# One Trainium2 core, a state-space layer beside a Mish layer: layer-norm statistics moved behind size maxima, and half of the C copies, weight scalings and weight sums moved to other places of the instruction order

## The chip, the cores and the metric

The kernel runs on one core of a Trainium2 chip. The time is the device time of one execution in microseconds (us), and lower is better. Five engines work side by side, each through its own list of instructions in order: TensorE (PE, matmuls into eight PSUM banks), VectorE (DVE), ScalarE (ACT), GpSimd (POOL) and SyncE (SP, which only issues DMAs here). ACT and POOL issue DMAs too. An instruction that waits holds up everything behind it on its engine.

## The reference

x has 2048 rows of 1024 values. It is normalized by row, and the result goes through two branches that are added to x: a diagonal complex recurrence with input matrix B and output matrix C (1024 states), and a dense layer to 3584 features with Mish, followed by a dense layer back to 1024.

```python
xn = _layernorm(x, axis=-1)
# state-space branch
Lam_bar = jnp.exp(dt * Lam)
B_bar = ((Lam_bar - 1.0) / Lam)[:, None] * Bmat
Bu = jnp.einsum("bld,pd->blp", xn + 0j, B_bar)
for t in range(L):
    h = Lam_bar[None, :] * h + Bu[:, t, :]
y = 2.0 * jnp.einsum("blp,dp->bld", hseq, Cmat).real + xn * Dskip[None, None, :]
# dense branch
h = jnp.einsum("bsd,df->bsf", xn, w1) + b1
act = h * jnp.tanh(softplus(h))
return x + y + jnp.einsum("bsf,fd->bsd", act, w2)
```

## The kernel before

**Blocks.** The 2048 rows are worked in four blocks of 512 (`blk` 0 to 3). Each block has the same stages on TensorE: dense 1 (28 tiles f of 128 features, `first_tile`, L816, one PSUM bank per tile, f modulo 8), the projection with B (`project_in` in block 0, `project_fast` later), dense 2 (`dense`, called in `tail`, L1182), and the projection with C (`proj`, L1182 too), whose output units are added to x and stored (`finish`, L1251; `store`, L1243).

**Fast products.** From block 1 on the B projection uses sums of blocks of the operands in place of some products, so that seven products of half size do the work of eight (`product`, L880). For blocks 2 and 3 dense 1 does the same with W1 (`w_product`, L950). This needs scaled copies and sums of the weights, in float16, made while blocks 0 and 1 run.

- For W1 there are seven groups of 512 features, 0 to 6. `w_load(i)` (L1024) has POOL load group i raw, four DMAs into the scratch buffers `hb` or `act`. `w_scale(i)` (L1085) has ACT scale it in place by two activations, and POOL store three of the four pieces to DRAM (`w_store`, L1079). `w_sums(i)` (L1097) has VectorE form four sums, each stored by POOL. The scale comes from size maxima: for groups 3 to 6 VectorE reads the ring of weights in block 0 (`w_most`, L1044) and `w_row(0)` spreads them; groups 0 to 2 are measured by ACT in block 1 (`w_abs`, L1035, `w_row(1)`).
- For B and C the scale of each state comes from sizes of B (`rows_size`, `rows_scale`). `rows_C(j)` (L1341, its store L1343) has ACT write a scaled copy of row group j of C into four tiles of `act` and then store that to DRAM, from ACT's own DMA queue. `scale_B` (L1350) and `sums_B` (L1361, L1362) have VectorE scale B and form its sums, which are written over the memory of the C rows that have been copied.

**The order.** Every engine's list is written out by hand. The call order in the Python code is the order on each engine; a helper (`Queue`, `Buf`) derives the semaphore waits from what each operation reads and writes. `side(f)` is called after the tile f of dense 1 and puts other work there. The strings HEAD, HEAD1, WHOLE and SEVEN hold the order of a later block's projection, one word for each step: a letter a to d with a digit is a product of a pair of row groups and its evacuation, r a rotation, u the first matmuls of a unit of dense 2, k `w_sums`, n `w_load`. Block 1 uses WHOLE, blocks 2 and 3 SEVEN.

**Statistics.** x of block 1 is loaded by POOL during block 0's dense 1; `ln_stats_only` (L517, L519) forms mean and variance of a quarter of it on VectorE, four calls. They are needed when the first recurrence of block 0 is done (`ln_root`).

**Weights and the ring.** W1, W2 and the scaled C come through a ring of seven slots filled by SP (L408, L411). A slot is refilled when TensorE, and in block 0 `w_most`, have read it. SP also issues the transposing loads of B (L793) and C (L799), in order with the ring's loads.

**The recurrence.** `recur` (L1147 to L1157) runs on VectorE, eight row groups in a block; in block 0 VectorE and ACT also scale a row group of C behind each (`scale_C`, L780 to L787).

Of the kernel before, what the change touches and what calls it, by code (L numbers as in the profile page):

```python
# [163 lines left out]
def build_kernel(nc, A_x, A_Lambda_re, A_Lambda_im, A_B_re, A_B_im, A_C_re, A_C_im,  # L164
# [9 lines left out]
    NJ = NP // P  # L174
# [6 lines left out]
    FAST = 1  # L181
# [1 line left out]
    SPLIT = range(2, NB)  # L183
    GROUPS = ((0, 7), (7, NPL), (NPL, NPL + 8), (NPL + 8, NF))
    HEAD = "a2 a1 b2 b1 a5 b5 a6 b6 a3 b3 a7 b7 c2 d2 a4 b4 c5 c1 r0 d5 d1 r1 c6 c3 d6"
    HEAD1 = HEAD.replace("a2 a1 b2 b1", "k5 a2 a1 b2 b1 k6").replace("c6 c3", "n0 n1 c6 c3")
    WHOLE = HEAD1 + " d3 c7 d7 u7 c4 r2 u5 d4 u6 u4 r3 r4 r5 r6 r7"
    LATE = (" a3 b3 a7 b7 c2 d2 a4 b4 c5 c1 d5 d1 c6 c3 d6"
            " d3 c7 w1 d7 w5 w2 c4 d4 w6 r0 x1 x5 x2 w7 w3 r1 x6 w4 y1 y5 y2 x7 x3 r2 y6 x4"
            " z1 z5 g2 z2 y7 y3 z6 y4 u0 z7 u2 z3 u1 z4 u7 g3 r3 r4 r5 r6 r7")  # L190
# [109 lines left out]
    def wsm(n, lo, hi):  # L300
        return cs[:, CN.index("den") + n, lo:hi]
# [212 lines left out]
    def ln_stats_only(blk, q):  # L514
        i, s = blk % 2, q % 2
        for h in range(2):
            vop(lambda e, h=h: e.bn_stats(stats[:, s, h, :], xx[:, i, q, h * 512:(h + 1) * 512]),  # L517
                reads=[b_xx[i][q]], writes=[b_stats[s]])
        vop(lambda e: e.bn_aggr(mv[:, q, :], stats[:, s, :, :]), reads=[b_stats[s]], writes=[b_mv[q]])  # L519
# [497 lines left out]
    def w_load(i):  # L1017
        sem = DmaSem(nc, "d_wraw%d" % i, nper=4)
        for ci in range(2):
            for kh in range(2):  # L1020
                dst, b_dst = w_unit(w_raw(i, ci, kh))
                f0 = (4 * i + 2 * ci) * P
                src = B_w1[kh * NH * P:(kh + 1) * NH * P, f0:f0 + 2 * P].rearrange("(k p) f -> p k f", p=P)
                PO.dma(lambda e, dst=dst, src=src: e.dma_start(dst.rearrange("p (k f) -> p k f", k=NH), src),  # L1024
                       sem, writes=b_dst)
# [56 lines left out]
    def w_scale(i):  # L1082
        for ci in range(2):
            t, b_t = w_half(i, ci)
            aop(lambda e, t=t: e.activation(t, t, AF.Copy, scale=wsm(2, i, i + 1)),  # L1085
                reads=b_t + [b_wsm[2][i]], writes=b_t)
        for n, ci, kh in ((1, 0, 0), (2, 0, 1), (4, 1, 1)):
            w_store(i, n, *w_unit(w_raw(i, ci, kh)))
# [12 lines left out]
    def project_fast(blk, order, open_unit):  # L1101
        keep = {}
        split = order is not WHOLE
        for o in order.split():
            kind, n = o[0], int(o[1:])
            if kind == "r":
                rotate_in(n)
            elif kind == "u":
                open_unit(n)
            elif kind == "g":  # L1110
                mish(blk, n)
            elif kind == "k":
                w_sums(n)
            elif kind == "n":
                w_load(n)
            elif kind in QUADS:
                w_product(blk, QUADS.index(kind), n)
                w_evacuate(blk, QUADS.index(kind), n, keep)
            else:
                product("abcd".index(kind), n)  # L1120
                evacuate("abcd".index(kind), n, keep, split or kind in "ab")
# [257 lines left out]
    for blk in range(NB):  # L1379

        def side(f):
            if blk:
                at = (8, 10, 12, 15)
                if f in at:
                    ln_skip(blk, at.index(f))
                    if blk >= FAST:
                        sums_x(at.index(f))
                if blk == FAST:
                    if f == 1:
                        rows_spread(1)  # L1390
                    if f == 0:
                        scale_B(0, (1,))
                    if f < 3:
                        scale_B(f + 1)
                    if f in (3, 4, 17, 19):
                        sums_B((3, 4, 17, 19).index(f))
                    if f == 4:
                        w_scale(4)
                    if f in (7, 11):
                        w_sums(3 + (f - 7) // 4)  # L1400
                    if f == 16:
                        w_load(5)
                        w_load(6)
                    if f in (21, 24):
                        w_scale(5 + (f - 21) // 3)
                return
            if f == 2:
                turn_sines()
            if f == NR:
                aop(lambda e: e.activation(act[:, 0:NR, 0:2 * P], hraw[:, 0:NR, :], AF.Mish),  # L1410
                    reads=b_hbf[0:4], writes=b_actf[0:NR])
            if f in (19, 27):
                for j in range(4):
                    table(j + (4 if f > 19 else 0))
            if f in (5, 6, 7, 8):
                coefficients(f - 5)
            if f in (8, 9, 11, 12):
                ln_skip(0, (8, 9, 11, 12).index(f))
            if f in (14, 16, 18, 20):
                ln_stats_only(1, (f - 14) // 2)  # L1420
            if f in turns:
                transpose_B(turns.index(f))
            if f >= 26:
                transpose_C(f - 26)
            if f >= 4 * ROWS[0][0] and f % 4 < 2:
                w_most(f // 4, f % 4)
            if f == 26:
                w_row(0)

        for f in range(0 if blk in SPLIT else NF):  # L1430
            first_tile(blk, f)
            side(f)

        near = 0 < blk < NB - 1
        out_stage = tail(blk, n_item[0] + (len(W_ITEMS) if blk in SPLIT else 0))
        open_unit = next(out_stage)
        if blk in SPLIT:
            if near:
                for q in range(NQ):
                    load_x(PO, blk + 1, q)  # L1440
            project_fast(blk, SEVEN, open_unit)
        elif blk:
            project_fast(blk, WHOLE, open_unit)
        else:
            project_in()
        if near and blk not in SPLIT:
            for q in range(NQ):
                next_stats(blk + 1, q)
            w_abs(0)
            w_abs(1)  # L1450
        for j in range(NJ):
            if blk == 0 and j == NJ - 1:
                rows_scale(0)
            recur(blk, j)
            if near and j == (5 if blk in SPLIT else 1):
                next_root()
                for q in range(NQ):
                    next_scale(blk + 1, q)
            if blk in SPLIT:
                if j == 1:  # L1460
                    next(out_stage)
                if near and j == 1:
                    for q in range(NQ):
                        next_stats(blk + 1, q)
                if near and j == 5:
                    for q in range(NQ):
                        transpose_dma(q)
                continue
            if blk:
                if j == 1:  # L1470
                    next(out_stage)
                    w_load(2)
                    w_abs(2)
                    w_row(1)
                if j == 6:
                    w_exponent(1)
                    for i in (0, 1, 2):
                        w_scale(i)
                continue
            if j == 0:  # L1480
                ln_root()
                w_exponent(0)
                for q in range(NQ):
                    ln_scale(1, q)
                next(out_stage)
                for i in range(NHS):
                    rows_load(i)
            scale_C(j)
            for i in {4: (0, 1, 2), 5: (3, 4, 5, 6), 6: (7, 8, 9, 10), 7: range(11, 16)}.get(j, ()):
                rows_size(i)  # L1490
        if near:
            for q in range(NQ):
                ln_skip(blk + 1, q)
            for n in range(4):
                sums_x(n, VE)
        if blk < NB - 1:
            carry()
        if blk == FAST:
            for i in (0, 1, 2):
                w_sums(i)  # L1500
        if blk == FAST - 1:
            rows_scale(1)
            vop(lambda e: e.tensor_tensor(qi[:], qi[:], c("ss").unsqueeze(1).to_broadcast([P, 2, NJ]), op=ALU.mult),
                reads=[b_qi] + b_ss, writes=[b_qi])
            rows_spread(0)
            scale_B(0, (0,))
            for j in range(NJ):
                rows_C(j)
            for i in (3, 4):
                w_load(i)  # L1510
            w_scale(3)
        for _ in out_stage:
            pass
        if blk == FAST - 1:
            snaps_ready()

    SP.wait(out_events.values())

# [33 lines left out]
```

## Time and profile before

| what | us |
|---|---|
| median of 3 runs (618.35 to 621.8) | 619.75 |
| the profiled execution | 617.87 |
| its span, first to last instruction | 616.3 |
| TensorE busy | 601.0 |
| VectorE busy | 476.8 |
| ACT busy | 278.6 |
| POOL busy | 122.6 |
| mean granted TensorE clock | 0.992 of full |

A busy TensorE is not TensorE at its peak, since matmuls are pipelined; the granted clock of a stretch says whether it ran at full speed. The stages of block 0 and 1 on TensorE, by the first matmul of each:

| stage | starts at |
|---|---|
| block 0, dense 1 (full tiles) | 21.91 |
| block 0, projection with B | 58.17 |
| block 0, dense 2 | 85.79 |
| block 0, projection with C | 135.59 |
| block 1, dense 1 | 163.61 |
| block 1, projection with B | 217.99 |
| block 1, dense 2 (after the first units) | 252.53 |

Over the whole span 132.95 MB are moved by DMA, a mean of 216 GB/s.

### The profile page before, as it was taken

The page shows a single profiled execution, that of the slowest core. Times are in us where ns is not written, and L with a number is a line of the kernel's source. Part 1 is how long each engine was busy: PE and PEld are TensorE (multiplying, and loading weights), DVE is VectorE, ACT ScalarE, POOL GpSimd, SP SyncE. Part 2 cuts the span into 40 slices and gives each one's busy share as a digit, 9 for nine tenths or more (in the row PEclk, how much of TensorE's full clock was granted, in tenths as well). Part 3 has the DMA queues.
Part 4 walks back from the last instruction along what each step waited for, and adds up shares of the span by engine and source line. Part 5 has one row for each costly group of instructions (what it writes and reads, how often), then busy time and mean ns, then how long its engine had stood idle before and what let it go on. Part 6 is the DMA issues. An engine that isn't in the chain of part 4 may idle for free.

```text
span 616.3 us, 9311 instructions
## 1 busy us (share of the span) xinstructions
PE 601.0 (98%) x3583; PEld 349.3 (57%) x3583; DVE 476.8 (77%) x748; ACT 278.6 (45%) x367; POOL 122.6 (20%) x162
## 2 busy tenths in 40 slices
PE   8999999999979979999999999999999999999998
PEld 7644444444434448544448888644446888844444
DVE  6958998999978747989994667599954577689923
ACT  4749604479876362693615615590303714620000
POOL 2899200220327744100251000000000000000000
PEclk9999999999999979999999999999999999999999
DMA  9996999992699986268999707765576805864421
GB/s 244 295 229 181 193 220 248 307 293 80 183 377 384 335 311 203 81 227 183 265 364 366 271 18 223 229 181 167 159 206 220 307 18 157 254 202 141 163 76 68
DMA packets 109669, 132.95 MB, mean 216 GB/s; under 512 B 54346, under 2 KB 69322, under 8 KB 109626
## 3 DMA queue, kind: packets, MB, share of 16 engines
q1 hardware_dynamic: 97168, 95.77, 54.1%
q0 software_dynamic: 8768, 28.26, 13.6%
q10 hardware_dynamic: 3690, 8.34, 3.6%
q8 instruction: 28, 0.46, 0.3%
q14 instruction: 15, 0.12, 0.1%
HBM read 99.04 MB, written 21.24 MB: 195 GB/s over the span
## 4 chain that ended last, share of the span: by engine, by line
PE 59%; DVE 16%; DMA 9%; SPq 6%; POOL 5%; issue 3%; ACT 2%; ACTq 0%; POOLq 0%; DVEq 0%
PE ps L1182 37%; PE ps L950 12%; PE ps L880 11%; SPq L799 4%; DVE hT L1147 3%; DMA xx<-in_A_x_dram 2%; DVE CT L787 2%; DMA wsd<-hb 2%; DVE CT L784 2%; DMA out_dram<-xx 2%; ACT snaps L970 2%; DVE hb L1097 2%; DVE mt L1152 1%; DVE cs L1044 1%; POOL py L709 1%
## 5 line engine op out<-in xcount | busy, mean ns | idle before, releaser
L1182 PE MATMUL ps<-ring,act 128*128 128x512 bf16 x704 | 153.2, 379 | 1.2 <-DVE mt L1133 1.2
L1182 PEld LDWEIGHTS ps<-ring,act 128*128 128x128 bf16 x704 | 68.8, 98 | 84.0 <-issue 1.7
L816 PE MATMUL ps<-xnT,ring 128*128 128x512 bf16 x392 | 86.8, 384 | 4.4 <-ACT act L824 4.2
L970 ACT ACTIVATE snaps<-ps,par,cs 128x256 f32<-128x256 f32 x80 | 43.3, 562 | 99.6 <-PE ps L950 49.9
L1182 PE MATMUL ps<-ring,hT 128*128 128x512 bf16 x378 | 82.1, 379 | 0.0
L816 PEld LDWEIGHTS ps<-xnT,ring 128*128 128x128 bf16 x392 | 38.6, 99 | 52.2 <-issue 7.6
L1182 PEld LDWEIGHTS ps<-ring,hT 128*128 128x128 bf16 x378 | 37.0, 98 | 44.6
L1147 DVE TENSOR_TENSOR_SCAN hT<-cs,qi,hT 128x512 bf16<-128x512 f32 x48 | 58.9, 1268 | 0.0
L950 PE MATMUL ps<-TT,ring 128*128 128x256 f16 x448 | 55.8, 273 | 0.4 <-ACT snaps L970 0.4
L950 PEld LDWEIGHTS ps<-TT,ring 128*128 128x128 f16 (+1 forms) x448 | 43.7, 98 | 6.8 <-issue 0.9
L1182 PE MATMUL ps<-ring,hb 128*128 128x512 bf16 x192 | 43.1, 379 | 0.5 <-DVE act L973 0.5
L950 PE MATMUL ps<-xnT,ring 128*128 128x256 bf16 x336 | 42.9, 273 | 0.0
L824 ACT ACTIVATE act<-ps,par 128x512 bf16<-128x512 f32 (+1 forms) x56 | 33.8, 670 | 19.1 <-PE ps L816 19.1
L1152 DVE TENSOR_TENSOR mt<-hT,tab 128x1024 bf16<-128x1024 bf16 x64 | 41.4, 687 | 1.1
L950 PEld LDWEIGHTS ps<-xnT,ring 128*128 128x128 bf16 (+1 forms) x336 | 32.9, 98 | 4.7
L1085 ACT ACTIVATE hb<-hb,cs 128x2048 bf16<-128x2048 bf16 x12 | 23.3, 1998 | 24.5 <-DVE cs L1074 15.6
L1251 DVE TENSOR_TENSOR xx<-ps,xx 128x1024 bf16<-128x1024 f32 (+1 forms) x16 | 18.7, 1187 | 18.3 <-PE ps L1182 18.3
L987 DVE SCALAR_TENSOR_TENSOR act<-ps,cs,snaps 128x512 bf16<-128x512 f32 x24 | 18.0, 751 | 17.2 <-PE ps L950 15.7
L846 DVE TENSOR_TENSOR mt<-hT,tab 128x1024 bf16<-128x1024 f16 x48 | 30.9, 685 | 0.4
L1097 DVE TENSOR_TENSOR hb<-hb 128x1024 f16<-128x1024 bf16 (+1 forms) x24 | 17.6, 735 | 17.6 <-DMA wsd<-hb 17.0
L1182 PEld LDWEIGHTS ps<-ring,hb 128*128 128x128 bf16 x192 | 18.6, 98 | 22.0 <-DMA ring<-in_B_w_dram 1.5
L1079 POOL DMA_DIRECT2D wsd<-hb x42 | 22.7, 543 | 40.1 <-ACT hb L1085 30.7
(184 smaller groups left out, 873.8 us busy)
## 6 DMA issues: line engine op xcount, KB each, us to landing
ring<-in_B_w_dram SPq DMA_DIRECT2D x84, 512.0 KB, 4.8
ring<-wsd SPq DMA_DIRECT2D x98, 256.0 KB, 4.3
ring<-ctd SPq DMA_DIRECT2D x24, 512.0 KB, 3.3
wsd<-hb POOLq DMA_DIRECT2D x42, 256.0 KB, 4.8
hb<-in_B_w_dram POOLq DMA_DIRECT2D x24, 256.0 KB, 5.5
ctd<-act ACTq DMA_DIRECT2D x8, 512.0 KB, 5.6
out_dram<-xx ACTq DMA_DIRECT2D x15, 256.0 KB, 4.9
xx<-in_A_x_dram POOLq DMA_DIRECT2D x12, 256.0 KB, 6.3
```

The costliest lines, as they stand in the source:

```text
L799: SP.dma(lambda e: e.dma_start_transpose(CT[:, :, ci, db * P:(db + 1) * P], src[db * P:(db + 1) * P, :]), s_CT, writes=b_CT + b_early)
L816: PE.mm(lambda e, k=k, w=w: e.matmul(ps[:, bank, :], lhsT=w, rhs=xnT[:, k, :], start=k == 0, stop=k == NK - 1), reads=[b_ring[s]] + b_xnT, ...
L824: aop(lambda e: e.activation(at[0][:, ts], ps[:, bank, ts], AF.Mish, bias=b1(f)), reads=[b_ps[bank], b_par], writes=[at[1]])
L846: vop(lambda e, s=s: e.tensor_tensor(mt[:, s, :, :], hT16[:, :, j, :], tab[:, s, j, :].unsqueeze(1).to_broadcast([P, 2, TB]), op=ALU.mult) ...
L880: PE.mm(lambda e, w=w, x=x, o=o, begin=begin, end=end: e.matmul(ps[:, bank, o:o + TH], lhsT=w, rhs=x, start=opens and begin, stop=end, ski ...
L950: PE.mm(lambda e, w=w, x=x, o=o, begin=begin, end=end: e.matmul(ps[:, bank, o:o + TH], lhsT=w, rhs=x, start=opens and begin, stop=end, ski ...
L970: aop(lambda e, o=o, p=p, j=j: e.activation(o, p, AF.Identity, scale=ig, bias=b1(f0 + j)), reads=[b_ps[b], b_par, b_ig], writes=b_dst)
L1085: aop(lambda e, t=t: e.activation(t, t, AF.Copy, scale=wsm(2, i, i + 1)), reads=b_t + [b_wsm[2][i]], writes=b_t)
L1097: vop(lambda e, o=o, x=x, y=y, op=op: e.tensor_tensor(o.bitcast(f16), x, y, op=op), reads=b_x + b_y, writes=b_o)
L1147: vop(lambda e, ci=ci, init=init: e.tensor_tensor_scan(out=hT[:, ci, j, :], data0=cj("r", j).to_broadcast([P, TB]), data1=hT[:, ci, j, :], ...
L1152: vop(lambda e, s=s: e.tensor_tensor(mt[:, s, :, :], hT[:, :, j, :], tab[:, s, j, :].unsqueeze(1).to_broadcast([P, 2, TB]), op=ALU.mult), ...
L1182: PE.mm(lambda e: e.matmul(ps[:, u, :], lhsT=lhsT, rhs=rhs, start=st_, stop=last), reads=reads, writes=[b_ps[u]], first=st_, last=last, te ...
```

## The change

In block 0, the four calls of `ln_stats_only` move from the tiles 14, 16, 18 and 20 of dense 1 to 23, 25, 26 and 27, so that most of the eight size maxima (tiles 12, 13, 16, 17, 20, 21, 24 and 25) come before them on VectorE.

At the end of block 0, four of the eight C copies stay, and the other four move to the tiles 6 to 9 of block 1's dense 1. There the scaling of group 3 moves from the end of block 0 to tile 2 and that of group 4 from tile 4 to tile 5; the sums of groups 3 and 4 from tiles 7 and 11 to 10 and 14; the loads of groups 5 and 6 from tile 16 to 18. The scalings of groups 5 and 6 move from tiles 21 and 24 to the beginning of the projection (v5 and v6, a new kind of step). The sums of group 5 (k5) move from the beginning of the projection to the place ahead of c6, those of group 6 (k6) and the loads of groups 0 and 1 (n0, n1) to the place behind the rotation r3. `snaps_ready`, which only hands on which copies must be done before the projection's scratch is written, goes along. No arithmetic is added or removed.

```diff
-    HEAD1 = HEAD.replace("a2 a1 b2 b1", "k5 a2 a1 b2 b1 k6").replace("c6 c3", "n0 n1 c6 c3")
-    WHOLE = HEAD1 + " d3 c7 d7 u7 c4 r2 u5 d4 u6 u4 r3 r4 r5 r6 r7"
+    HEAD1 = "v5 v6 " + HEAD.replace("c6 c3", "k5 c6 c3")
+    WHOLE = HEAD1 + " d3 c7 d7 u7 c4 r2 u5 d4 u6 u4 r3 k6 n0 n1 r4 r5 r6 r7"
...
+            elif kind == "v":
+                w_scale(n)
...
-                    if f == 4:
-                        w_scale(4)
-                    if f in (7, 11):
-                        w_sums(3 + (f - 7) // 4)
-                    if f == 16:
+                    if f in (2, 5):
+                        w_scale(3 + f // 5)
+                    if 6 <= f < 10:
+                        rows_C(f - 2)
+                    if f == 10:
+                        snaps_ready()
+                    if f in (10, 14):
+                        w_sums(3 + (f - 10) // 4)
+                    if f == 18:
                         w_load(5)
                         w_load(6)
-                    if f in (21, 24):
-                        w_scale(5 + (f - 21) // 3)
...
-            if f in (14, 16, 18, 20):
-                ln_stats_only(1, (f - 14) // 2)
...
+            if f in (23, 25, 26, 27):
+                ln_stats_only(1, (23, 25, 26, 27).index(f))
...
-            for j in range(NJ):
+            for j in range(4):
                 rows_C(j)
             for i in (3, 4):
                 w_load(i)
-            w_scale(3)
         for _ in out_stage:
             pass
-        if blk == FAST - 1:
-            snaps_ready()
```

## The prediction

> **What bounds the kernel now.** I read the page's engine totals first, then TensorE's waits, the windows around them, and last the timelines of the engines that it waits for. All times are us from the start of the span.
>
> ```profile
> PE 601.0 (98%) x3583; PEld 349.3 (57%) x3583; DVE 476.8 (77%) x748; ACT 278.6 (45%) x367; POOL 122.6 (20%) x162
> ...
> PE ps L816 <- ACT act L824: 4.2, 1, 4.2
> PE ps L880 <- ACT act L824: 4.1, 1, 4.1
> PE ps L1182 <- DVE mt L1133: 1.2, 1, 1.2
> ```
>
> TensorE sets the end, its work is unchanged, so only its waits and slow clock can be won. Two of three large waits are for Mish on ACT. The windows (TensorE's busy time first, then its granted clock, DMA share and GB/s last) show a second price:
>
> ```profile
> 90.00:95.00 5.00, 3.78 (x18) 1.55 (x17) 4.83 (x7) 0.00 (x0) 0.00 (x0) 1.00 1.01 190
> 180.00:185.00 5.00, 3.23 (x9) 1.25 (x10) 2.10 (x4) 4.99 (x7) 1.00 (x2) 0.72 1.05 402
> 225.00:230.00 5.00, 5.00 (x26) 3.45 (x24) 4.86 (x8) 0.02 (x1) 1.70 (x4) 0.50 0.72 273
> ```
>
> After the 1.2 wait the clock stays 1.00; after each wait above 4 it falls. The 160 dense-1 matmuls from 181.77 to 217.99 took 36.2 where 160 x 0.217 (27.79 for 128, block 0's projection) is 34.7: 1.5 lost. The 48 matmuls from 224.00 to 232.3 took 8.3 where 48 x 0.109 (16 in 1.75, from 234.22) is 5.2: 3.1 lost. With a 0.2 wait for VectorE at 163.6, there is 1.2 + 0.2 + 4.2 + 1.5 + 4.1 + 3.1 = 14.3 to win.
>
> What ACT did before the two waits (start, duration, idle time and its releaser in brackets):
>
> ```profile
> 170.24 2.00 ACT L1341 ACTIVATE act<-CT,cs 128x2048 bf16<-128x2048 bf16 x1 [0.40 <-ACT act L1341]
> ...
> 175.73 2.00 ACT L1085 ACTIVATE hb<-hb,cs 128x2048 bf16<-128x2048 bf16 x1 [3.49 <-DMA hb<-in_B_w_dram]
> ...
> 213.88 3.90 ACT L1085 ACTIVATE hb<-hb,cs 128x2048 bf16<-128x2048 bf16 x2 [5.37 <-DMA hb<-in_B_w_dram]
> ```
>
> Eight C copies end at 172.2, the scaling of group 3 waits for its raw weights, and the first Mish starts at 180.9, though its tile was ready at 165.4. Near the end of dense 1 the scalings of groups 5 and 6 again sit in front of Mish while their loads land.
>
> **Part 1, the statistics (block 0).** VectorE stood still for x, and SP behind it, because a ring slot can't be reloaded before its size maximum is read:
>
> ```profile
> 47.91 1.42 DVE L517 BATCH_NORM_STATS2 stats<-xx 128x6 f32<-128x512 bf16 x2 [8.88 <-DMA xx<-in_A_x_dram]
> ...
> 41.27 3.23 SPq L793 DMA_TRANSPOSE BT<-in_A_B_im_dram  x1
> 53.33 2.55 SPq L411 DMA_DIRECT2D ring<-in_B_w_dram  x2
> ```
>
> Afterwards six maxima of 2.2 run from 34.6 to 47.8, just when x lands; two more and four statistics of 1.5 end at 58.3 instead of 67.3. VectorE then follows the projection on TensorE (pair 1 done at 58.17 + 16 x 0.217 = 61.6; 3.47 a pair against VectorE's 3.28) and ends its last pair at 86.0 + 3.3 = 89.3, not 93.4. The wait of 1.2 goes. SP goes on at 44.5 instead of 53.3, and all B and C transposes behind it move up: by 8.8 if the queue alone decides, by 5.2 if the DMA engines do (their share was 0.33 and 0.38 in 48 to 56, so 8 x 0.65 was free). C then lands by 96.4 instead of 101.6. VectorE needs it after the first recurrence and the exponents and scalings of x (4.4 + 4.0), at 97.7 instead of 103.1. From there to 160.5 its timeline has no gap over 0.3, so the chain ends at 155.1, 5.4 earlier; ACT's C scalings wait on it and move along. POOL's loads of groups 3 and 4 start at 160.0 instead of 165.4. TensorE itself starts dense 1 only 1.4 earlier, at 162.2.
>
> **Part 2, half of the C copies and the scalings in dense 1.** ACT does four copies (2.0, and 0.4 to issue the store) from 147.9 to 157.5, then queues four output stores, the last after VectorE's last sum at 164.1 (TensorE ends that unit at 162.2). Table load 1.3, three Mish of 0.6, the third after its tile at 167.4: ACT reaches the scaling of group 3 at 168.1. Its four loads landed 10.3 after the first issue before; now 9, since half of the C stores are gone, so 169.0 (up to 170.3). Two scalings 3.9, three Mish, two scalings of group 4: 178.7. Mish 6, copy 4, Mish 7, copy 5: 184.7. Mish 8 overwrites the buffer that copy 4 stores from, so ACT, with copies 6 and 7 and every later Mish queued behind, waits for that store: issued at 181.7, landed L later. Mish 8, copy 6, Mish 9, copy 7, Mish 10 then take 6.6. TensorE needs the bank of Mish 10 for tile 18, at 162.2 + 18 x 1.746 = 193.6. The stall is 181.7 + L + 6.6 - 193.6 = L - 5.3. Stores of C took 2.6 to 9.2 (5.2 and 6.0 when issued at 162.7 and 165.1, 8.2 when at 167.5): from nothing to 3.9. I take 7.1, the mean of the last two, since the stage is as full of DMA: 1.8, in pieces under 3, the waits of tiles 17 and 18. The wait of 4.2 and its 1.5 go. The ring is next in line: loads issued at 170.8 took 15.4, and the same slot is needed 14.8 after its issue now that no stall covers it; with fewer stores beside it I cost this at nothing, 0.6 if the cover is gone.
>
> The Trainium skill speaks against this move: by "DMA: Bandwidth & Descriptors", section "Issuing engines are not separate DMA queues", transfers issued from different engines share the same 16 DMA engines, so spreading the stores wins issue time only. The share of 1.05 above agrees; by that rule alone L would be the 9.2 and the stall 3.9.
>
> POOL's queue: group 3's three stores (0.54 each) now come behind the four loads of x for block 2, which wait for output stores (landing by 173). Group 3's sums on VectorE come at 181.7, after the remaining scalings and sums of B; stores issued by 174.6 land in 5.8, so nothing. The remaining B sums now wait for copies 5 and 7 (ACT, about 194.6) and end near 197.4, well before the first product that uses them (c5, 226.8). Loads of groups 5 and 6 go out near 195 to 201 and land by 208.
>
> **Part 3, groups 5 and 6 scaled behind the last Mish.** Dense 1 ends at 162.2 + 28 x 1.746 + 1.8 = 212.9; the last Mish at 213.6; the scalings (4 x 1.95) end at 221.4. ACT is next needed after the seventeenth product, c5, 212.9 + 17 x 0.873 = 227.7. Nothing is lost, and the wait of 4.1 with its 3.1 goes. If the loads, landed by 208, came 10 later, the scalings would end at 225.8 and still be in time.
>
> **Part 4, the sums of group 5 among the products.** These stood where TensorE was waiting or slow; now they sit on VectorE between a rotation and the sums that free a bank:
>
> ```profile
> 247.22 2.47 DVE L905 TENSOR_TENSOR hT<-ps,snaps 128x512 f16<-128x512 f32 x4
> ...
> 249.49 1.04 PE L880 MATMUL ps<-TT,BT 128*128 128x256 f16 x8
> ```
>
> The third of these four sums ends at 249.07 and lets product c4 start at 249.49: slack 0.4. Four sums of weights take 2.9 (2.8 to 3.9 in the timeline), so c4 waits 2.4 (to 3.5); d4 and the open units follow without another wait. The sums' own wait, for the stores of the scaled weights (issued by 218.5, landing in 5.8), ended long before. The group 6 sums (2.9, four POOL stores) and POOL's loads of groups 0 and 1 come after rotation 3. Relative to TensorE, VectorE is 5.8 - 2.4 = 3.4 late through the recurrence, hidden by dense 2: the last recurrence ended at 302.9, its row is used after 315. At the end of the block the sums of groups 0 to 2 ended at 320.4 and four additions of 1.2 follow; TensorE needs the fourth after seven products of block 2. Nothing there; without this cover it would be the 3.4.
>
> On the clock: the gaps that I add are 2.4 and less; the rows have 1.00 after 1.2 and a loss after 4.1, so 0 to 3.1, and I take 0, nearer to the first. "TensorE: Matmul & The Clock Gate", section "Why this matters for your kernels", wants idle gaps kept below about 3 us; by it c4 costs no clock, and a stall of 3.9 in one piece would.
>
> **Sum.** 14.3 - 1.8 - 2.4 = 10.1. The profiled execution took 617.87 (span 616.3 and 1.6 around it), which would become 607.8. The runs' median, 619.75, lies 1.9 above it; taken from that it is 609.65, rounded to 609.5.
>
> **Rivals.** (a) The new stalls don't come: stores land in 5 and VectorE runs ahead. 619.75 - 14.3 = 605.5. For it: stores of 2.6 to 5.2; against: c4's slack of 0.4. (b) The gaps at c4 or tile 18 pass the length that costs clock: 3.9 + 3.5 + 3.1 instead of 4.2, so 616.0. For it: the DMA share of 1.05. (c) The change doesn't do what it says: transposes are held by the DMA engines, whose share is about 1 from 56 to 105, and C lands no earlier. The scaling of group 3 then starts at 175.7 instead of 169.0, so the stall is 1.8 + 6.7 = 8.5, with 1.5 of clock, and the 0.2 stays: 619.75 - 14.1 + 8.5 + 1.5 + 2.4 = 618.1. (d) Slower: the stores of copy 4 land as late as ring loads do. At L = 15.4 the stall is 10.1, with 2.3 of clock (between 1.5 and 3.1): 619.75 - 14.3 + 2.4 + 12.4 = 620.3, and from there on it is slower; at L = 18 it is 622.9, 0.5% over. Against it: no store of ACT's queue took over 9.2.
>
> **How the numbers follow.** Forecast 0.56, (a) 0.14, (b) 0.17, (c) 0.07, (d) 0.06. The range reaches from 604.5, below (a), to 615, nearly (b). A change of 0.5% (3.1) is about the least that a measurement here can tell: faster 0.87, same 0.08, slower 0.05.
>
> **What would show it.** In the profile after: no idle VectorE before the statistics; C's first scaling near 97; the first Mish of block 1 near 165.5; a short wait of TensorE for Mish in dense 1; the projection starting near 213 at clock 1.00; a wait of about 2.4 for the sums at c4. A long TensorE wait for a ring load, or for Mish behind a C store, would prove me wrong.

## The result and the profile after

The changed kernel took 612.56 us in the median of 20 runs (610.59 to 626.21). The kernel before, run beside it on the same chip, took 620.12 (615.77 to 623.3, 20 runs). The ratio is 0.988, with a 95% interval of 0.986 to 0.991: 1.2% faster. The run of 626.21 had a mean granted clock of 0.949 and stands outside the ratio. The profiled execution took 612.65 (span 611.1, mean clock 0.997) where that of before took 617.87.

TensorE's waits in the changed kernel (what was waited for, total us, how often, the longest):

```profile
PE ps L950 <- DVE xx L1253: 2.9, 1, 2.9
PE ps L880 <- DVE hT L905: 2.3, 1, 2.3
PE ps L816 <- ACT act L824: 1.6, 2, 1.1
...
PE ps L950 <- ACT snaps L970: 1.0, 2, 0.8
```

Both large waits for Mish and the wait of 1.2 for VectorE in block 0 are gone. Of Mish 1.6 is left (forecast 1.8), the wait for the sums at c4 is 2.3 (forecast 2.4), and the first line is one that the forecast does not have: the first products of block 2 wait for the last additions of block 1 (`finish`; from there on the lines of the changed kernel stand two higher, so L1251 is now L1253).

The windows of the changed kernel, columns as in the prediction (the clock is the third number from the end):

```profile
190.00:195.00 5.00, 3.43 (x16) 1.28 (x15) 4.86 (x6) 4.19 (x5) 3.60 (x6) 1.00 0.97 357
...
235.00:240.00 5.00, 2.71 (x18) 1.42 (x17) 4.93 (x9) 0.47 (x1) 1.87 (x4) 1.00 0.56 210
...
315.00:320.00 5.00, 2.06 (x15) 1.59 (x15) 4.93 (x6) 0.00 (x0) 2.10 (x4) 0.88 0.96 296
320.00:325.00 5.00, 5.00 (x37) 4.09 (x36) 1.99 (x3) 2.82 (x6) 0.00 (x0) 0.78 1.04 410
```

The waits for Mish and the one at c4 lie in the first two rows: TensorE stands still there, but in this execution the clock stays 1.00. After the wait at the start of block 2 it falls to 0.88 and 0.78. The first 48 matmuls of block 2 took 6.90 (317.99 to 324.89) where before they took 5.24 (325.91 to 331.15): 1.7 lost on top of the wait.

The timeline of ACT in the changed kernel, block 1's dense 1 and the first part of its dense 2:

```profile
165.74 2.09 ACT L824 ACTIVATE act<-ps,par 128x512 bf16<-128x512 f32 x3
170.56 3.90 ACT L1085 ACTIVATE hb<-hb,cs 128x2048 bf16<-128x2048 bf16 x2 [2.73 <-DMA hb<-in_B_w_dram]
...
182.46 0.33 ACTq L1345 DMA_DIRECT2D ctd<-act  x1
...
187.94 0.69 ACT L824 ACTIVATE act<-ps,par 128x512 bf16<-128x512 f32 x1 [2.52 <-DMA ctd<-act]
...
259.28 3.62 ACT L1035 ACTIVATE CT<-hb 128x4096 bf16<-128x4096 bf16 x1 [5.50 <-DMA hb<-in_B_w_dram]
...
264.50 3.62 ACT L1035 ACTIVATE CT<-hb 128x4096 bf16<-128x4096 bf16 x1 [1.51 <-DMA hb<-in_B_w_dram]
```

The first Mish starts at 165.74 instead of 180.9. The store of copy 4 goes out at 182.46, and Mish 8 behind it waits until it has landed, 5.4 later. The scalings of groups 5 and 6 (left out here) run from 212.78 to 220.4. The last two rows are the size measures of groups 0 and 1 for the next block: both wait for raw weights that POOL now loads late. In the kernel before they ran without a wait, since POOL issued the loads in one go as soon as the sums were stored, long ahead of ACT:

```profile
233.13 5.94 POOL L1024 DMA_DIRECT2D hb<-in_B_w_dram  x8 [0.38 <-issue]
```

The same loads on POOL in the changed kernel, behind the stores of the sums of group 6:

```profile
247.21 3.72 POOL L1024 DMA_DIRECT2D hb<-in_B_w_dram  x5 [0.38 <-issue]
251.60 2.22 POOL L1024 DMA_DIRECT2D hb<-in_B_w_dram  x3 [0.66 <-DMA wsd<-hb]
```

And VectorE in the changed kernel:

```profile
48.18 1.42 DVE L517 BATCH_NORM_STATS2 stats<-xx 128x6 f32<-128x512 bf16 x2 [0.37 <-DMA xx<-in_A_x_dram]
...
97.38 0.75 DVE L784 SCALAR_TENSOR_TENSOR CT<-CT,cs,ct 128x512 bf16<-128x512 bf16 x1
...
233.73 2.86 DVE L1097 TENSOR_TENSOR hb<-hb 128x1024 f16<-128x1024 bf16 x4
...
243.03 2.86 DVE L1097 TENSOR_TENSOR hb<-hb 128x1024 f16<-128x1024 bf16 x4
...
269.86 0.18 DVE L549 RECIPROCAL ln<-ln 128x4 f32<-128x4 f32 x1 [6.61 <-ACT ln L547]
...
313.84 2.86 DVE L1097 TENSOR_TENSOR act<-act 128x1024 f16<-128x1024 bf16 x4
```

The wait for x fell from 8.88 to 0.37, and C is scaled from 97.38 on (forecast 97.7). The two groups of sums stand at 233.73 and 243.03. At 269.86 VectorE waits 6.61 for the root of the next block's layer norm, which stands on ACT behind the two late measures. That wait was 2.69 before:

```profile
273.98 0.18 DVE L549 RECIPROCAL ln<-ln 128x4 f32<-128x4 f32 x1 [2.69 <-ACT ln L547]
...
320.36 2.35 DVE L1251 TENSOR_TENSOR xx<-ps,xx 128x1024 bf16<-128x1024 f32 x2
```

**Where the time went.** Of the 14.3 that was to win, all came. Paid were 1.6 (Mish), 2.3 (c4) and at the start of block 2 2.9 of wait, 1.7 of clock and 0.6 more of waits for ACT's copies out of the banks (1.0 instead of 0.4). 14.3 - 1.6 - 2.3 - 5.2 = 5.2, which is the difference of the two profiled executions. By the medians it is 7.6: the profiled execution of the kernel before lies 2.3 under its median, that of the changed kernel on it. The 1.7 of clock is not in every execution either. The profiled execution, with its one fall, has a mean clock of 0.997. Of the twenty runs nine have 0.997, with a median of 612.69, and ten have 1.000, with a median of 612.07.

### The profile page after: what moved, and what is told of

Same layout as the page of the kernel before. It is cut to its first block, busy times and chain, and to the rows that moved or that the text cites. A ratio compares the mean times of both kernels' runs of the same rounds, so it can differ in the third digit from the quotient of the medians.

```text
span 611.1 us, 9309 instructions
## 1 busy us (share of the span) xinstructions
PE 597.5 (98%) x3583; PEld 348.3 (57%) x3583; DVE 475.3 (78%) x748; ACT 278.4 (46%) x367; POOL 122.7 (20%) x162
## 5 line engine op out<-in xcount | busy, mean ns | idle before, releaser
L816 PE MATMUL ps<-xnT,ring 128*128 128x512 bf16 x392 | 85.3, 380 | 1.6 <-ACT act L824 1.6
L895 DVE COPY snaps<-ps 128x512 f32<-128x512 f32 x30 | 20.0, 686 | 19.8 <-PE ps L880 19.5
L1253 DVE TENSOR_TENSOR xx<-ps,xx 128x1024 bf16<-128x1024 f32 (+1 forms) x16 | 18.5, 1187 | 18.8 <-PE ps L1184 18.8
```

What stands on the lines that cost most here:

```text
L816: PE.mm(lambda e, k=k, w=w: e.matmul(ps[:, bank, :], lhsT=w, rhs=xnT[:, k, :], start=k == 0, stop=k == NK - 1), reads=[b_ring[s]] + b_xnT, ...
L1253: vop(lambda e: e.tensor_tensor(xr, src, xr, op=ALU.add), reads=b_ps[bank:bank + n] + [b_x], writes=[b_x])
```

## The experiments

Each was timed beside the kernel before on the same chip. "After" is the changed kernel.

**1. The statistics alone.** The kernel before with only this:

```diff
-            if f in (14, 16, 18, 20):
-                ln_stats_only(1, (f - 14) // 2)
...
+            if f in (23, 25, 26, 27):
+                ln_stats_only(1, (23, 25, 26, 27).index(f))
```

> The kernel before with only the statistics moved. My theory: C lands 5.4 us earlier in the chain of VectorE and ACT, so the waits at 92.9 (1.2) and 163.6 (0.2) go and the first Mish of block 1 starts near 175.7 instead of 180.9; the first large wait (4.2 and 1.5 of clock) shrinks below 0.5. The second wait, for Mish behind the scalings of groups 5 and 6, stays at 4 to 5.6 with about 3 of clock. Time 613 to 615 against 620.1. Rival, statistics are hidden work: only the 1.2 goes, 618.7 or more.

615.03 (614.59 to 615.78, 6 runs); before 620.49; ratio 0.989 (0.985 to 0.993). The waits of 1.2 and 0.2 in block 0 went, ACT's first use of C came at 96.05 instead of 101.66, and the first wait for Mish fell from 4.2 to 1.4. But TensorE's largest waits were now:

```profile
PE ps L880 <- ACT act L824: 7.5, 1, 7.5
PE ps L880 <- DVE snaps L895: 1.7, 1, 1.7
PE ps L816 <- ACT act L824: 1.4, 1, 1.4
```

The wait at the end of dense 1 grew from 4.1 to 7.5: ACT waited 8.51 for the raw weights of group 5 with the last Mish behind it. What was won ahead of dense 1 was in part lost again at its end, since a scaling that waits for a load still stood in front of Mish.

**2. All but the statistics.** After, with the statistics back in their old place:

```diff
+            if f in (14, 16, 18, 20):
+                ln_stats_only(1, (f - 14) // 2)
...
-            if f in (23, 25, 26, 27):
-                ln_stats_only(1, (23, 25, 26, 27).index(f))
```

> The changed kernel with the statistics back in their old places, so block 1's part alone. My theory: the raw weights of group 3 land near 175 as before, ACT is some 5 us later in dense 1 than in the changed kernel, and TensorE waits for Mish of tiles 16 to 18 for 5 to 8.5 instead of 1.6, with 1.5 of clock; c4's wait of 2.3 and the wait of 2.9 at block 2's start stay. Time 617 to 620. Rival, block 1's part needs no help from block 0: 614, which is the changed kernel's 612.6 plus 1.4.

618.05 (616.65 to 621.08, 12 runs); ratio 0.995 (0.992 to 0.998). ACT's first use of C came at 101.84, as late as before, the wait of 1.2 in block 0 was there, and the waits for Mish came to 4.8. The separate gains by the medians, 5.5 for the statistics and 2.4 for the rest, add up to 7.9, and together they bring 7.6: each part brings about as much without the other as with it.

**3. The load of group 0 earlier.**

```diff
-    HEAD1 = "v5 v6 " + HEAD.replace("c6 c3", "k5 c6 c3")
-    WHOLE = HEAD1 + " d3 c7 d7 u7 c4 r2 u5 d4 u6 u4 r3 k6 n0 n1 r4 r5 r6 r7"
+    HEAD1 = "v5 v6 " + HEAD.replace("c6 c3", "k5 n0 c6 c3")
+    WHOLE = HEAD1 + " d3 c7 d7 u7 c4 r2 u5 d4 u6 u4 r3 k6 n1 r4 r5 r6 r7"
```

> The changed kernel with the four loads of group 0 issued right behind the sums of group 5 instead of behind those of group 6. My theory: the wait of 2.9 for VectorE at block 2's start, its slow clock (1.7) and 0.6 of further waits come from the loads of groups 0, 1 and 2 going out together beside the ring's loads, landing 7 to 10 after their issue instead of 4.6, which makes ACT measure late and VectorE idle for the root (6.6). Now group 0 lands by 245, the idle time before the root falls below 3, the wait at block 2 goes: 607.5 to 609. Rival, VectorE is late because of the sums of groups 5 and 6 themselves (5.7 of work): the wait stays, 612 to 613.

610.58 (608.71 to 617.52, 6 runs); ratio 0.983 (0.978 to 0.988): between the two. In the profile the root's wait fell to 1.79 and the wait at the start of block 2 was gone, as the theory has it. Another came in its place, 2.0 for a ring load of derived weights (`wsd`) at 337, and in that execution, the slowest of the six, C landed late in block 0.

**4. The sums of group 5 later**, with group 6 and the loads left where they are:

```diff
-    HEAD1 = "v5 v6 " + HEAD.replace("c6 c3", "k5 c6 c3")
-    WHOLE = HEAD1 + " d3 c7 d7 u7 c4 ...
+    HEAD1 = "v5 v6 " + HEAD
+    WHOLE = HEAD1 + " d3 c7 d7 k5 u7 c4 ...
```

> The changed kernel with the sums of group 5 behind d7 instead of ahead of c6. The wait at c4 (2.3) goes in every theory. My theory: TensorE then comes to block 2 2.3 earlier while VectorE ends no sooner, so the wait there grows from 2.9 to about 5.2 and the slow clock stays or grows: 612 to 614, no gain. Rival, waits add up: 610.3.

611.0 (609.43 to 615.31, 6 runs); ratio 0.983 (0.979 to 0.988). The wait at c4 was gone, and the wait at the start of block 2 grew from 2.9 to 4.0. A stall of TensorE had hidden a part of VectorE's lateness; without it the lateness showed up later. It grew by 1.1 and not by the 2.3 that was expected, since the wait for the root was shorter here, 5.27 instead of 6.61, and the median is nearer to the rival's 610.3.

**5. C copies 4 to 7 four tiles later** in what they overwrite (f0 of the last four slots).

```diff
-        f0 = (16, 20, 0, 4, 8, 12, 16, 20)[j]
+        f0 = (16, 20, 0, 4, 12, 16, 20, 24)[j]
```

> The changed kernel with the four late C copies written to act tiles 12, 16, 20 and 24 on instead of 8, 12, 16 and 20 on, so that Mish of tile 8 no longer waits for the store of copy 4. My theory: the two waits of TensorE for Mish at tiles 17 and 18 (0.5 and 1.1) go and everything behind moves up with them: 611.0 against 612.6. Rival, ACT is late by its work alone (the copies, not the store): the waits stay, 612.6.

611.07 (609.14 to 620.71, 6 runs); ratio 0.982 (0.978 to 0.986). The theory's number. ACT no longer waited for the stores of its copies, yet the waits for Mish came to 2.7 in the profile: there the scaling of group 3 began 2.8 later (173.35) than in after. Kernels in which that scaling starts about equally late tell the store and ACT's work apart:

| kernel | tiles of the copies | scaling of group 3, after the start of dense 1 | waits for Mish |
|---|---|---|---|
| after | old | 8.80 | 1.6 |
| 8 | old | 8.86 | 1.8 |
| 7 | old | 9.97 | 3.3 |
| 11 | new | 9.46 | 0.3 |
| 6 | new | 10.16 | 1.0 |
| 5 | new | 12.24 | 2.7 |

At an equal start the store costs some 2, which covers the 1.6 of after; the 2.7 of this profile come from ACT's late start.

**6. The three together**: the slots of experiment 5, k5 and n0 both behind d7, and k6 and n1 behind r3:

```diff
-    HEAD1 = "v5 v6 " + HEAD.replace("c6 c3", "k5 c6 c3")
-    WHOLE = HEAD1 + " d3 c7 d7 u7 c4 r2 u5 d4 u6 u4 r3 k6 n0 n1 r4 r5 r6 r7"
+    HEAD1 = "v5 v6 " + HEAD
+    WHOLE = HEAD1 + " d3 c7 d7 k5 n0 u7 c4 r2 u5 d4 u6 u4 r3 k6 n1 r4 r5 r6 r7"
```

> The changed kernel with three edits together: group 0 loaded behind the sums of group 5, these sums behind d7, and the C copies' tiles moved on. My theory: 5.2 at block 2's start, 2.3 at c4 and 1.6 in dense 1 go: 612.6 - 9.1 = 603.5. Rival, VectorE's sums themselves make it late: only the 1.6 goes, 611.

609.96 (609.27 to 611.58, 6 runs); ratio 0.981 (0.977 to 0.985): a clear miss of the 603.5. The start of block 2 in this kernel's timeline, TensorE and POOL:

```profile
252.61 0.76 POOL L1024 DMA_DIRECT2D hb<-in_B_w_dram  x1 [6.84 <-DMA wsd<-hb]
...
314.63 1.87 PE L950 MATMUL ps<-xnT,ring 128*128 128x256 bf16 x8 [3.39 <-DVE xx L1253]
```

Group 0 came in time, but POOL's load of group 1 waited for the stores of group 6's sums, landed at 261, and the root waited 4.58. So two things add up on VectorE: the sums themselves and the measures behind the loads.

**7. The root ahead of the measures**: `w_abs(0)` and `w_abs(1)` moved behind `next_root` and `next_scale`:

```diff
-            w_abs(0)
-            w_abs(1)
...
                 next_root()
                 for q in range(NQ):
                     next_scale(blk + 1, q)
+                if blk not in SPLIT:
+                    w_abs(0)
+                    w_abs(1)
```

> The changed kernel with ACT's size measures of groups 0 and 1 moved behind the root and the scalings of x, the loads left where they are. My theory: the late loads cost time only since the root queues behind the measures on ACT; now VectorE doesn't wait 6.6 for the root, though it may wait some 2 to 4 later for the scales of groups 0 to 2. The wait of 2.9 at block 2's start and its clock go: 607.5 to 609. Rival, VectorE's sums make it late: 612.6.

611.53 (610.09 to 615.42, 6 runs); ratio 0.984 (0.980 to 0.988). The root's wait was gone, but VectorE then waited 5.03 for the spread maxima (`wmx`), which hang on the same measures:

```profile
292.50 0.67 DVE L1069 TENSOR_REDUCE cs<-wmx 128x3 f32<-128x384 f32 x1 [5.03 <-DMA wmx<-wmd]
```

The lateness was passed on by one step.

**8. The sums where VectorE stands still.** Group 5 and the load of group 0 behind b7, group 6 and the load of group 1 behind d7:

```diff
-    HEAD1 = "v5 v6 " + HEAD.replace("c6 c3", "k5 c6 c3")
-    WHOLE = HEAD1 + " d3 c7 d7 u7 c4 r2 u5 d4 u6 u4 r3 k6 n0 n1 r4 r5 r6 r7"
+    HEAD1 = "v5 v6 " + HEAD.replace("a7 b7 c2", "a7 b7 k5 n0 c2")
+    WHOLE = HEAD1 + " d3 c7 d7 k6 n1 u7 c4 r2 u5 d4 u6 u4 r3 r4 r5 r6 r7"
```

> The sums of group 5 and the load of group 0 stand behind b7, where VectorE waited 1.93 and 1.67; the sums of group 6 and the load of group 1 stand behind d7. Theory (VectorE is late at the start of block 2 because the sums of groups 5 and 6 push the loads of groups 0 and 1 back, and the chain of measures, root and recurrence behind them): the wait of 2.29 at c4 goes, and so do most of the 2.94 at L1253 and its 1.7 of clock: 612.6 - 2.3 - 2.9 - 1.7 = 605.7, so 605 to 608. Rival (what is late is the work of VectorE itself, 5.8 us of it, wherever it stands, or group 1's load lands late as in the earlier variant): the wait at L1253 stays at 2.5 to 3.5 and only c4's goes: 609.5 to 611.

605.16 (604.06 to 607.82, 6 runs); before 622.09 on this chip; ratio 0.975 (0.971 to 0.978). The theory's number. TensorE waited neither at c4 nor for the additions; VectorE's timeline in this kernel:

```profile
223.15 2.86 DVE L1097 TENSOR_TENSOR hb<-hb 128x1024 f16<-128x1024 bf16 x4
225.93 1.28 DVE L922 CAST hT<-ps 128x512 f16<-128x512 f32 x2
228.40 0.69 DVE L905 TENSOR_TENSOR hT<-ps,snaps 128x512 f16<-128x512 f32 x1 [1.19 <-ACT snaps L897]
...
236.00 2.86 DVE L1097 TENSOR_TENSOR hb<-hb 128x1024 f16<-128x1024 bf16 x4
...
260.39 0.17 DVE L549 RECIPROCAL ln<-ln 128x4 f32<-128x4 f32 x1
...
309.90 1.22 DVE L1253 TENSOR_TENSOR xx<-ps,xx 128x1024 bf16<-128x1024 f32 x1 [0.41 <-PE ps L1184]
```

The first group of sums fits into idle time: a gap of 1.93 is filled, and behind it VectorE still waits, 1.19 instead of 1.67, so it is on time again. VectorE no longer waits for the root at all; and at the end of the block it is VectorE that waits for TensorE.

**9. Without the sums.** After, with `w_sums` reduced to its stores for groups 5 and 6:

```diff
-            vop(lambda e, o=o, x=x, y=y, op=op: e.tensor_tensor(o.bitcast(f16), x, y, op=op),
-                reads=b_x + b_y, writes=b_o)
+            if i < 5:
+                vop(lambda e, o=o, x=x, y=y, op=op: e.tensor_tensor(o.bitcast(f16), x, y, op=op),
+                    reads=b_x + b_y, writes=b_o)
             w_store(i, n, o, b_o)
```

> The kernel after, with the eight additions and subtractions of groups 5 and 6 left out; their stores, their waits for the scaled weights and the loads of groups 0 and 1 behind them stay in their places, so a part of the projection's weights of the next block is wrong. It measures what the 5.8 us of VectorE cost in all. If the sums' time is the whole cause: c4's wait of 2.3 and the wait at L1253 with its clock (4.6) go, 605 to 606.5. If the late and crowded loads of groups 0 and 1 are the cause of the wait at L1253: the loads still go out only behind rotation 3, 5.8 earlier at best, the root waits 2 to 5 longer than before, and 608 to 610 remain.

603.83 (603.07 to 608.67, 6 runs); ratio 0.973 (0.970 to 0.977), somewhat below what either side expected. It doesn't split the sums from the loads: without sums to wait for, POOL had the loads out from 224.90, and the root's wait was 2.66 again. It gives the whole price: 8.7 for 5.7 us of VectorE's work in the places where the change put it, of which experiment 8 wins back 7.4.

**10. The sums of group 2 behind the last additions:**

```diff
         if blk == FAST:
-            for i in (0, 1, 2):
+            for i in (0, 1):
                 w_sums(i)
...
         for _ in out_stage:
             pass
+        if blk == FAST:
+            w_sums(2)
```

> The kernel after, with the four sums of group 2 moved behind the four additions of L1253, so that the additions start 2.9 earlier. Theory (the wait at L1253 and the loss of clock behind it cost 4.6): the first addition ends at 315.0, when TensorE arrives; the wait goes and 612.6 becomes 608 to 609. Rival (the lateness is only passed on: group 2's stores, issued near 322 instead of 317, hold the ring's loads): the same time as after, 612 to 613, with a wait for ring<-wsd later in block 2.

612.79 (609.1 to 614.84, 6 runs); ratio 0.986 (0.982 to 0.989). TensorE's waits:

```profile
PE ps L816 <- ACT act L824: 3.9, 2, 2.9
PE ps L880 <- DVE hT L905: 2.3, 1, 2.3
PE ps L950 <- DMA ring<-wsd: 1.9, 1, 1.9
```

The wait for the additions is gone, and the one for the ring that the rival named stands there, with 1.9. The larger wait for Mish belongs to this execution, in which x and C landed late in block 0, which the edit leaves alone. By the median nothing was won; how much of the 4.6 came back as the ring's wait can't be told from it.

**11. Experiments 5, 8 and 10 together**, the three diffs in one kernel (the expectation's first and third variants are experiments 8 and 10).

> The first and the third of these variants together, and copies 4 to 7 of C four tiles later in dense 1. If the waits add up as terms: after 612.6 minus 2.3 (c4) minus 4.6 (L1253 and clock) minus about 1 (Mish), 604 to 606. If block 2 starts on time in the first variant already, this one equals it within 1.5. If the lateness comes back as a wait of the ring's loads for group 2's stores: 608 or more.

603.98 (603.03 to 604.91, 5 runs); ratio 0.972 (0.969 to 0.975). The fastest that leaves no work out, 8.6 below the median of the changed kernel, and not to be told from experiment 8 by the intervals. The wait for Mish is down to 0.3 and no wait for VectorE's sums or additions is left.

## Why the prediction was right, and the step that failed

The forecast of 609.5 (604.5 to 615) holds the 612.56, and the sign was right. Set against the profiled execution, 607.8 was forecast and 612.65 measured, 4.9 more: of the 10.1 that were to come, 5.2 came there and 7.6 by the medians. By its steps:

| step | forecast | measured |
|---|---|---|
| VectorE ends the last pair of block 0's projection | 89.3 | 89.06 |
| VectorE scales C from | 97.7 | 97.38 |
| loads of groups 3 and 4 start | 160.0 | 159.64 |
| dense 1 of block 1 starts | 162.2 | 161.76 |
| first Mish of block 1 | 165.5 | 165.74 |
| scaling of group 3 starts | 169.0 | 170.56 |
| store of copy 4 lands after | 7.1 | 5.4 |
| waits for Mish in dense 1 | 1.8 | 1.6 |
| projection of block 1 starts | 212.9 | 211.99 |
| wait at c4 | 2.4 | 2.3 |
| start of block 2, wait and clock | 0 | 5.2 |

**Part 1** held in its mechanism, and experiment 1 shows it alone. That the times agree so well is partly luck: with the same block 0 VectorE's scaling of C began anywhere from 96.78 to 103.14 in the profiles of experiments 3 to 11. **Part 2** held in its mechanism, the store of copy 4 in front of Mish 8, as experiment 5 shows; its number is right because errors cancel. The raw weights of group 3 took 10.9 from their first issue (159.64) to the scaling at 170.56, not 9, so the scaling starts 1.6 later. Of that 0.8 is left when the store goes out (182.46), TensorE is 0.4 earlier than forecast, and the store lands 1.7 sooner, although the DMA share from 180 to 185 is 1.05 as before: that share alone did not make L the 9.2. **Part 3** held: the scalings behind the last Mish cost nothing.

**The step that failed** is the one on the sums of group 6 and the loads of groups 0 and 1 behind rotation 3: "Relative to TensorE, VectorE is 5.8 - 2.4 = 3.4 late through the recurrence, hidden by dense 2 ... Nothing there; without this cover it would be the 3.4." The cover was real, but the lateness was mis-sized, and the step looked at the fourth addition where the first one decides: its bank is the one that the first product of block 2 takes (in experiment 10 block 2 starts at 320.68, ahead of the fourth addition at 320.88). In the kernel before, the first addition of L1251 ended near 321.5 and TensorE took its bank at 325.91: some 4.2 to spare after the 0.2 that the hand-over takes. 3.4 would have been hidden. But the loads, issued at 247.21 instead of 233.13 (35.2 instead of 15.1 after the projection's first matmul), made ACT's measures and with them the root late, and VectorE's wait for the root grew by 6.61 - 2.69 = 3.9. Together VectorE was 7.3 late, 3.1 more than the cover. The loads had been named in the step and given no price; the profile puts them at 3.9.

The same account can be set against the experiments: lateness from the sums, plus the growth of the root's wait over 2.69, less the cover of 4.2, less the clock that TensorE itself lost behind c4 (the last section has the rows). The sums are 2 x 2.86 = 5.7, less 2.3 where TensorE stalls at c4 as well; in experiment 8 the first group fits into idle time, so 2.9 is left. In experiment 7 the root's wait is gone (-2.7), and 5.0 for the maxima came instead.

| kernel | sums | growth of the wait | clock behind c4 | what is left | wait at L1253 in the profile |
|---|---|---|---|---|---|
| after | 3.4 | 3.9 | 0 | 3.1 | 2.94 |
| 4, group 5 later | 5.7 | 2.6 | 0 | 4.1 | 4.03 |
| 5, slots | 3.4 | 3.6 | 0 | 2.8 | 2.65 |
| 6, three together | 5.7 | 1.9 | 0 | 3.4 | 3.39 |
| 2, no statistics | 3.4 | 2.3 | 1.5 | 0.0 | none |
| 7, root first | 3.4 | 2.3 | 1.5 | 0.0 | none |
| 3, load of group 0 earlier | 3.4 | -0.9 | 1.5 | below 0 | none |
| 8, sums where VectorE stands still | 2.9 | -2.7 | 0 | below 0 | none |

Experiments 4 and 6 tell the theory apart from its rivals: the sums alone would make 4 and 6 equal, and the loads alone (a growth of 1.9 in 6, less than the cover) would leave no wait in 6. Both fail, and their sum fits within 0.2. In experiments 2 and 7 no wait is left only because TensorE was 1.5 late itself. In these two TensorE's waits for ACT's copies at the start of block 2 came to 2.7 and 2.6 instead of 0.4; what they hang on was not followed further.

**The clock** was the second part of the miss in the profile. It was put at 0 for gaps of 2.4 and less. In the profile of after c4's gap of 2.29 cost none, but that was luck: the same gap cost 1.5 in experiments 2, 3, 7 and 10. The gap of 2.9 that was not foreseen cost 1.7.

**The rivals.** (a), in which no new stall comes, fell with the wait at c4. (b) asked for a gap long enough to cost clock at c4 or tile 18; in after there was one, but elsewhere, and the time lies between the forecast and (b); at c4 it came in four of the experiments. (c) did not come in after, since C landed by 94.6; experiment 2 is that case, and its 618.05 agrees with the 618.1, though by a different sum (4.8 for Mish instead of 8.5, and more in block 2). (d) did not come: the store of copy 4 landed in 5.4.

## What to carry to other kernels

When work is moved into a busy engine's list, price what is queued behind it on every engine, loads included, and follow it to the next hand-over: lateness from two sources adds up, and only the sum may be held against the cover. Removing one stall of the bounding engine can uncover the same lateness later, as experiments 4 and 7 show. The cheap place for a few microseconds of work is an idle gap of that engine in the trace; putting one group of sums wholly into such a gap, placing the other ahead of c4 and sending the loads out early was worth another 7.4 here.

## What the runs showed of the hardware

**Gaps and the clock.** At one place, the start of block 2, the first 48 matmuls take 5.24 at full clock. After a gap of 2.65 (experiment 5) they took 6.90, after 2.94 (after) 6.90, after 3.39 (experiment 6) 8.08 and after 4.03 (experiment 4) 6.80. The loss does not simply grow with the gap: it was 1.6 to 2.8, the least of it after the longest. Shorter gaps are less certain. The gap at c4 was 2.28 to 2.30 in six profiles. In after and in experiment 5 the clock from 236 to 248 was 1.00, in experiments 2, 3, 7 and 10 it was 0.86 to 0.90, and from c4 to the start of block 2 TensorE needed 78.1 instead of 76.60, its waits left out: 1.5 lost. The same two groups in after and in experiment 7:

```profile
238.45 1.05 PE L880 MATMUL ps<-TT,BT 128*128 128x256 f16 x8 [2.29 <-DVE hT L905]
239.33 1.46 PE L1184 MATMUL ps<-ring,act 128*128 128x512 bf16 x6
```

```profile
239.90 1.57 PE L880 MATMUL ps<-TT,BT 128*128 128x256 f16 x8 [2.29 <-DVE hT L905]
241.26 2.66 PE L1184 MATMUL ps<-ring,act 128*128 128x512 bf16 x6
```

A gap of 2.58 in dense 1 (experiment 2) cost nothing, and one of 1.97 (experiment 3, for the ring) took the clock to 0.50 between 338 and 340. In the profiles here, from 30 us on, no gap up to 1.9 cost any clock, all from 2.65 on did, and those between did so in five of eight cases. The bound of about 3 us in the Trainium skill ("TensorE: Matmul & The Clock Gate", section "Why this matters for your kernels") is thus too generous here.

**Loads beside other loads.** The raw weights of groups 0 and 1 went out between 247 and 254 in after. From issue to landing they took 8.9 in the median, and the ring's loads issued between 245 and 262 took 12.7, where over the whole execution the loads into `hb` took 7.5 and those of the ring 5.1. In the kernel before, where no ring load went out between 233 and 240, the same loads took 4.6.

**The same block 0, other landings.** In after and in experiments 3 to 11 block 0's instructions are the same, but the first use of C by ACT varied from 94.6 to 101.7 between the profiled executions. In one of the late ones (experiment 10) VectorE waited 4.31 for x instead of 0.37, and one of SP's transposes beside it took 8.20 instead of 4.28. With it go the start of dense 1 (161.0 to 163.6) and the waits for Mish, so single profiles can differ by several microseconds for reasons that no edit made.
